# Products and transposes of a fused attention and gated convolution in 32-column strips or whole, after what stands before them, in a new TensorE order

## The chip, the cores and the metric

The kernel runs on one core of a Trainium2 chip. The metric is the device time of one execution in microseconds. Three runs of the kernel before gave 411.37, 413.17 and 414.0 us, so the median is 413.17.

## The reference

Four batches of 12800 rows of 128 channels go through agent attention with 49 agents, and its result through a gated convolution. All arrays are float32.

```python
def sm(a, b):
    s = scale * (a @ b.transpose(0, 2, 1))
    s = s - s.max(-1, keepdims=True)
    e = np.exp(s)
    return e / (e.sum(-1, keepdims=True) + 1e-09)
agent_v = sm(agents, k) @ v              # 49 x 128 per batch
x = sm(q, agents) @ agent_v              # 12800 x 128 per batch
...
for k in range(K):                       # 5 taps, causal
    gate_pre += conv_w[k][None, None, :] * xp[:, k:k + S, :]
gate = 1.0 / (1.0 + np.exp(-gate_pre))
out = gate * (x @ w_val) @ w_out
```

## The kernel before, in words

**Units and chunks.** The keys, values and queries of a batch are cut into 10 units of 1280 rows; the output into 25 chunks of 512 rows per batch, numbered 0 to 100 over the four batches (the last one is split in two). Nothing of `x` is ever written: the agents' values are folded into the weights of the convolution. `x` is a weighted sum over agents, so the gate is a product of the query weights with a folded table (five taps and rests), and so is the value.

**The kinds of work on TensorE**, with the letters of the order table:

- `k` and `q` (`key_scores`, `queries`, through `score_matmuls`, L411): scores of a unit of keys or queries against the agents. They are float32, in column strips: four matmuls of 32 columns (`tile_position=(0, g * BLK)`) take a quarter of the unit each, for two halves of the agents. A float32 matmul stands as two in the trace, so a unit is 16. They write one of two PSUM banks `sc` in turn.
- `v` (`agent_values`, L552): exponentials of the keys' scores times the values, summed in the bank `av`. For batches 1 to 3 they are strips of 32 columns as well, for batch 0 they are 64 columns wide. A unit is 40 matmuls in the trace (20 in batch 0).
- `f` (`fold_weights`, five steps a batch: L606 and L610, L655, L741, L771, L797): normalises the agents' values, multiplies them with `w_val`, splits the results into 16-bit high and low parts in `wst` and `wsp`, and turns them with 16-bit transposes; `wo` is turned as float32 (L771).
- `m`, `n`, `j` (`key_max`, L469 and L484; `regroup`, L521): the maximum over the keys of a batch, turned with two small float32 transposes.
- `t` (`transposes`): turns the query weights `pt` of a unit into `x`. The first four units go through TensorE (L929), the others by a DMA that transposes, issued on SyncE's queue (L915).
- `g` (`gates`, L1008 and L1012): six 16-bit matmuls of 128 columns by 512 rows for a chunk's gate; `a` (`values`, L1035 and L1039): two for its value; `o` (`project`, L1080 to L1082): three for its output.

**Around them.** ScalarE copies key scores out of `sc`, takes exponentials, the tanh `th` of a gate, the 16-bit copy `hh` of `h` and the copy of an output into `ob`. VectorE takes maxima, transposes blocks and makes `h = (th + 1) * val`. GpSimd makes the rest `hl = h - hh` and weighs queries. An out product needs `hh` and `hl` of its chunk.

**What sets the order.** TensorE's order is a table of numbers written out by hand (`order`, L1185 to L1208). The other engines' orders come from `Plan.order`, a list scheduler that runs once over all steps with estimated costs and adds 0.12 us to TensorE's clock wherever the key of a step differs from that of the step before (L153 to L157). Loads go through SyncE's queue into a ring of eleven buffers `ld`, in the order in which the table's `k`, `q` and `v` need them; transposing DMAs, shifted copies (L968) and outputs (L1116) share that queue.

Of the kernel before, what the change touches and what calls it, by code (L numbers as in the profile page):

```python
# [17 lines left out]
P = 128  # L18
G = 4
# [50 lines left out]
class Plan:  # L70
# [25 lines left out]
    def order(self, held=None):  # L96
# [32 lines left out]
        while done < n:  # L129
# [23 lines left out]
            if e == "pe":  # L153
                here += 1
                if key != kind:
                    when += 0.12
                kind = key  # L157
            else:
                queues[e].remove(i)
# [31 lines left out]
def tile_agent_attention_gated_conv(  # L191
# [37 lines left out]
    mrep = const.tile([2, G, BLK], F32, name="mrep")  # L229
# [28 lines left out]
    def small(b):  # L258


        if b:
            return av, "av"
        turn[1] += 1
        return ((outp, "out"), (val, "val"), (gate, "gate"))[turn[1] % 3]

# [35 lines left out]
    nc.vector.memset(fac, 0.0)  # L301
    for t in wst_sb:
        nc.gpsimd.memset(t[:, TAPS + 1 :, :], 0.0)
# [104 lines left out]
    def score_matmuls(b, src, out):  # L408
        for j in range(2):
            for g in range(G):  # L410
                nc.tensor.matmul(  # L411
                    out=out[g * BLK : (g + 1) * BLK, j, 0:GT],
                    lhsT=ag_sb[:, b, j * BLK : (j + 1) * BLK],
                    rhs=src[:, g * GT : (g + 1) * GT],
                    start=True,
                    stop=True,
                    tile_position=(0, g * BLK),
                )
# [35 lines left out]
    def key_max(b, units=range(NU), bias=None):  # L454
# [14 lines left out]
            lambda: nc.tensor.transpose(out=p1[0:2, 0:P], in_=m2, identity=ident),  # L469
# [3 lines left out]
        def spread():  # L473
            rows = p1[0:2, 0:P].rearrange("j (g a) -> j a g", g=G)
            nc.vector.tensor_reduce(
                out=mrep, in_=rows.unsqueeze(1).to_broadcast([2, G, BLK, G]),
                axis=AX.X, op=ALU.max,
            )
# [5 lines left out]
            lambda: nc.tensor.transpose(  # L484
                out=p2[:, 0:2], in_=mrep.rearrange("j g a -> j (g a)"),
                identity=ident[0:2, 0:2],
            ),
# [11 lines left out]
    def regroup(b):  # L499


        p3, at3 = small(b)

        def differ():
            for j in range(2):
                r = slice(j * BLK, (j + 1) * BLK)
                nc.vector.tensor_tensor(
                    out=fac[r], in0=kbias[0][r, j : j + 1], in1=kbias1[r, j : j + 1],
                    op=ALU.subtract,
                )  # L510

        add("dve", 0.25, differ, [("kbias", 0), "kbias1"], ["fac"])
        add(
            "act", 0.2,
            lambda: nc.scalar.activation(out=fac[0:AP_], in_=fac[0:AP_], func=AF.Exp),
            ["fac"], ["fac"],
        )
        yield
        add(
            "pe", 0.2,  # L520
            lambda: nc.tensor.matmul(  # L521
                out=p3[:, 0:1], lhsT=twice,
                rhs=fac, start=True, stop=True,
            ),
            ["fac"], [at3], key="m",
        )
        add("dve", 0.12, lambda: nc.vector.tensor_copy(out=fac2, in_=p3[:, 0:1]), [at3], ["fac2"])

    def agent_values(b, u):
# [5 lines left out]
        cols, key = (BLK, "sc") if b else (AP_, "av")  # L535
# [11 lines left out]

        def matmuls(blocks):
            for n in blocks:
# [37 lines left out]
    def fold_weights(b):  # L587
# [17 lines left out]
        def normals():  # L605
            nc.tensor.matmul(  # L606
                out=pt[:, 0:AP_], lhsT=av2[:, C : C + 1].to_broadcast([P, P]), rhs=fold,
                start=True, stop=True,
            )
            nc.tensor.matmul(  # L610
                out=pt[:, AP_ : 2 * AP_], lhsT=av2[:, 0:C], rhs=fold,
                start=True, stop=True,
            )
# [25 lines left out]
        def gate_scale():  # L639
# [15 lines left out]
            lambda: nc.tensor.matmul(  # L655
                out=pv[:, 0:A], lhsT=wval_sb, rhs=avT, start=True, stop=True
            ),
# [81 lines left out]
        def transposes():  # L739
            for i in range(TAPS + 3):  # L740
                nc.tensor.transpose(  # L741
                    out=pw[:, i * P : (i + 1) * P], in_=wst[:, i, :], identity=ident16
                )
# [27 lines left out]
            lambda: nc.tensor.transpose(out=po[:, 0:P], in_=wo, identity=ident),  # L771
# [23 lines left out]
        def transposes2():  # L795
            for i in range(2):
                nc.tensor.transpose(  # L797
                    out=pq[:, i * P : (i + 1) * P], in_=wsp[:, i, :], identity=ident16
                )
# [107 lines left out]
    def transposes(b, u):  # L907
# [19 lines left out]
        def matmuls():  # L927
            for n in range(NBLK):
                nc.tensor.transpose(  # L929
                    out=ps[:, n // HB, n % HB * P : (n % HB + 1) * P], in_=pt[:, n, :],  # L930
                    identity=ident16,
                )
# [51 lines left out]
    def gates(t):  # L984
# [20 lines left out]
        def matmuls():  # L1005
            for k in range(TAPS):
                c = PAD - HALO + o2 + k
                nc.tensor.matmul(  # L1008
                    out=pg, lhsT=stat[:, k, :], rhs=x1[:, c : c + w],
                    start=(k == 0), stop=False,  # L1010
                )
            nc.tensor.matmul(  # L1012
                out=pg, lhsT=stat[0 : X2K, TAPS + 1, :],
                rhs=x2[0 : X2K, o2 : o2 + w], start=False, stop=True,
# [3 lines left out]
        add("pe", 1.3 * scale, matmuls, xs + x2k + st, [at_g], key="c")  # L1018
# [9 lines left out]
    def values(t):  # L1028
# [5 lines left out]
        def matmuls():  # L1034
            nc.tensor.matmul(  # L1035
                out=pv, lhsT=stat[:, TAPS, :], rhs=x1s[(b * NCH + n0 // CH) // 5 % NX][:, PAD + o2 : PAD + o2 + w],
                start=True, stop=False,
            )
            nc.tensor.matmul(  # L1039
                out=pv, lhsT=stat[0 : X2K, TAPS + 2, :],  # L1040
                rhs=x2[0 : X2K, o2 : o2 + w], start=False, stop=True,
# [25 lines left out]
    def project(t):  # L1067
# [11 lines left out]
        def matmuls():  # L1079
            nc.tensor.matmul(out=po, lhsT=wo16[:, 0, :], rhs=hh, start=True, stop=False)  # L1080
            nc.tensor.matmul(out=po, lhsT=wo16[:, 1, :], rhs=hh, start=False, stop=False)  # L1081
            nc.tensor.matmul(out=po, lhsT=wo16[:, 0, :], rhs=hl, start=False, stop=True)  # L1082

        if w < CH:
            add(
                "pe", 0.1 + 0.86 * scale,
                lambda: nc.tensor.matmul(out=po, lhsT=wo, rhs=h, start=True, stop=True),
# [86 lines left out]
    for t in range(len(chunks) + 2):  # L1174
# [108 lines left out]
```

## Time and profile before

| what | value |
|---|---|
| median of three runs | 413.17 us (411.37 to 414.0) |
| the profiled execution, its own time | 413.01 us |
| its span, first to last instruction | 411.3 us |
| mean granted TensorE clock | 0.994 |
| TensorE matmuls and weight loads in the trace | 3909 each |
| moved by DMA | 126.11 MB, mean 307 GB/s |
| last load used by TensorE | query unit 3.9, at 359.8 us |

A row of the profile names the line of the kernel, the engine (PE is TensorE, PEld its weight loads, DVE VectorE, ACT ScalarE, POOL GpSimd, SPq the queue of SyncE), the operation, what it writes and reads, the shape, a count, and times. `128*32 128x320 f32` is a matmul of 128 rows and 32 columns of the array, which streams 320 float32 columns. A matmul's end is modelled and its start is not, so starts are compared. In a timeline, rows that follow each other and are alike are merged under their first start; in the chain of waits, a piece lasts from its start to the start of the next one on the chain.

### The profile page before, as it was taken

The numbers are of one execution on the slowest core, as the hardware profiler recorded it, in microseconds if no ns is written. First come the engines' busy times: TensorE is split into PE (matmuls) and PEld (weight loads), VectorE is DVE, ScalarE is ACT, GpSimd is POOL, SyncE is SP. The second block draws the span as 40 slices with busy tenths as digits, with TensorE's granted clock in tenths as the row PEclk, the third lists the DMA queues.
The fourth block names the chain that finished last, engine by engine and source line by source line (L and its number), as shares of the span: only waits on it lengthen the run. The fifth ranks groups of instructions, "written<-read, shape, count | busy, mean of one in ns | idle before, by whom it ended". The sixth has DMA issues, their size and how long they took to land.

```text
span 411.3 us, 10037 instructions
## 1 busy us (share of the span) xinstructions
PE 396.3 (96%) x3909; PEld 196.1 (48%) x3909; DVE 259.8 (63%) x488; ACT 296.6 (72%) x523; POOL 286.5 (70%) x368
## 2 busy tenths in 40 slices
PE   4889999999999999999999999999999999999996
PEld 1339534445556444446555544445545544444442
DVE  7878787865777656367672668566756576553222
ACT  1476357778857877869887685798867678788875
POOL 6341558783799987752859594985788899999443
PEclk9989999999999999999999999999999999999999
DMA  8999999899999999999899999999999999996634
GB/s 315 421 416 409 358 380 368 251 288 297 412 335 294 380 300 328 310 362 376 304 272 365 314 390 249 316 223 382 247 382 262 295 251 327 247 228 135 193 124 158
DMA packets 74735, 126.11 MB, mean 307 GB/s; under 512 B 50400, under 2 KB 50784, under 8 KB 74688
## 3 DMA queue, kind: packets, MB, share of 16 engines
q1 hardware_dynamic: 74544, 125.34, 98.6%
q8 instruction: 31, 0.51, 0.5%
q10 hardware_dynamic: 144, 0.13, 0.2%
q14 instruction: 16, 0.13, 0.1%
HBM read 79.25 MB, written 26.21 MB: 256 GB/s over the span
## 4 chain that ended last, share of the span: by engine, by line
PE 88%; DVE 5%; DMA 3%; issue 1%; POOL 1%; ACT 1%; SPq 0%; DVEq 0%; POOLq 0%; ACTq 0%
PE gate L1008 26%; PE sc L411 19%; PE av L552 9%; PE out L1080 6%; PE val L1035 5%; PE val L1039 5%; PE gate L1012 5%; PE out L1081 5%; PE out L1082 5%; DMA ld<-kT 2%; DMA ld<-vP 1%; DVE kmx L446 1%; DVE ob L331 1%; DVE x L306 1%; DVE sT L421 0%
## 5 line engine op out<-in xcount | busy, mean ns | idle before, releaser
L1061 POOL TENSOR_TENSOR hl<-h,hh 128x512 f16<-128x512 f32 x99 | 114.8, 1162 | 61.2 <-ACT hh L1056 60.7
L1008 PE MATMUL gate<-x,stat 128*128 128x512 f16 (+1 forms) x500 | 124.3, 378 | 0.0
L1048 DVE SCALAR_TENSOR_TENSOR h<-th,val 128x512 f32<-128x512 f32 x100 | 68.3, 683 | 70.9 <-PE val L1039 41.4
L411 PE MATMUL sc<-ld,ag_sb 128*32 128x320 f32 x1280 | 99.4, 449 | 8.0 <-DMA ld<-kT 6.0
L1021 ACT ACTIVATE th<-gate,unscale 128x512 f32<-128x512 f32 x100 | 68.5, 685 | 28.0 <-PE gate L1012 22.6
L1101 ACT ACTIVATE ob<-out,oscale 128x512 f32<-128x512 f32 x98 | 67.3, 687 | 22.8 <-PE out L1082 20.2
L1008 PEld LDWEIGHTS <-stat 128*128 128x128 f16 x505 | 47.7, 98 | 61.0 <-issue 6.5
L1056 ACT CAST hh<-h 128x512 f16<-128x512 f32 x99 | 60.6, 613 | 16.1 <-DVE h L1048 15.6
L411 PEld LDWEIGHTS sc<-ld,ag_sb 128*32 128x32 f32 x1280 | 38.5, 112 | 56.1 <-issue 17.8
L829 POOL TENSOR_TENSOR qw<-sT,qmx 128x490 f32<-128x490 f32 x40 | 40.5, 1019 | 33.1 <-DVE qmx L824 32.9
L552 PE MATMUL av<-ld,eT 128*32 128x129 f32 (+1 forms) x1400 | 50.0, 274 | 0.8 <-DMA ld<-vP 0.8
L552 PEld LDWEIGHTS av<-ld,eT 128*32 128x32 f32 (+1 forms) x1400 | 43.7, 113 | 10.2 <-issue 4.7
L421 DVE STREAM_TRANSPOSE sT<-sc 128x640 f32<-128x640 f32 x40 | 33.8, 845 | 21.4 <-PE sc L411 16.6
L437 ACT COPY ks<-sc 128x640 f32<-128x640 f32 x40 | 27.6, 691 | 22.6 <-PE sc L411 14.6
L421 DVE STREAM_TRANSPOSE eT<-e 128x640 f32<-128x640 f32 x40 | 33.3, 839 | 15.9 <-ACT e L543 9.1
L874 POOL TENSOR_TENSOR pt<-qw,pt 128x480 f16<-128x480 f32 x40 | 42.6, 1072 | 0.5 <-ACT pt L860 0.4
L543 ACT ACTIVATE e<-ks,kbias 128x320 f32<-128x320 f32 x80 | 39.6, 552 | 4.0 <-DVE eT L421 3.6
L850 POOL TENSOR_TENSOR qw<-qw,qr 128x480 f32<-128x480 f32 x40 | 39.8, 996 | 3.3
L446 DVE TENSOR_REDUCE kmx<-ks 128x2 f32<-128x640 f32 x38 | 30.3, 805 | 14.8 <-ACT ks L437 14.5
L1035 PE MATMUL val<-x,stat 128*128 128x512 f16 x100 | 37.9, 379 | 0.2 <-DVE h L1048 0.2
L1012 PE MATMUL gate<-x,stat 106*128 106x512 f16 x100 | 38.0, 380 | 0.0
L1039 PE MATMUL val<-x,stat 106*128 106x512 f16 x100 | 37.9, 379 | 0.0
(155 smaller groups left out, 418.0 us busy)
## 6 DMA issues: line engine op xcount, KB each, us to landing
ld<-kT SPq DMA_DIRECT2D x40, 640.0 KB, 9.0
ld<-qT SPq DMA_DIRECT2D x40, 640.0 KB, 9.9
ld<-vP SPq DMA_DIRECT2D x39, 645.0 KB, 11.7
outT<-ob SPq DMA_DIRECT2D x48, 512.0 KB, 6.4
x<-x SPq DMA_DIRECT2D x18, 400.0 KB, 6.6
x<-x SPq DMA_DIRECT2D x4, 200.0 KB, 8.6
outT<-ob SPq DMA_DIRECT2D x3, 256.0 KB, 6.0
ld<-vP SPq DMA_DIRECT2D x2, 322.5 KB, 12.1
```

The source lines that it names most:

```text
L411: nc.tensor.matmul(out=out[g * BLK : (g + 1) * BLK, j, 0:GT], lhsT=ag_sb[:, b, j * BLK : (j + 1) * BLK], rhs=src[:, g * GT : (g + 1) * GT] ...
L421: nc.vector.transpose(out=out.rearrange("p n (j i) -> p j n i", j=2), in_=in_.rearrange("p j (n i) -> p j n i", i=BLK),)
L552: nc.tensor.matmul(out=av[o + j : o + j + cols, 0 : C + 1], lhsT=et[:, n, j : j + cols], rhs=vt[:, n, :], start=(opens and n < 2), stop=(c ...
L1008: nc.tensor.matmul(out=pg, lhsT=stat[:, k, :], rhs=x1[:, c : c + w], start=(k == 0), stop=False,)
L1012: nc.tensor.matmul(out=pg, lhsT=stat[0 : X2K, TAPS + 1, :], rhs=x2[0 : X2K, o2 : o2 + w], start=False, stop=True,)
L1021: lambda: nc.scalar.activation(out=th, in_=pg, func=AF.Tanh, scale=unscale[:, 0:1]),
L1035: nc.tensor.matmul(out=pv, lhsT=stat[:, TAPS, :], rhs=x1s[(b * NCH + n0 // CH) // 5 % NX][:, PAD + o2 : PAD + o2 + w], start=True, stop=False,
L1039: nc.tensor.matmul(out=pv, lhsT=stat[0 : X2K, TAPS + 2, :], rhs=x2[0 : X2K, o2 : o2 + w], start=False, stop=True,)
L1048: lambda: nc.vector.scalar_tensor_tensor(out=h, in0=th, scalar=1.0, in1=pv, op0=ALU.add, op1=ALU.mult),
L1056: "act", 0.18 + 0.43 * scale, lambda: nc.scalar.copy(out=hh, in_=h),
L1061: lambda: nc.gpsimd.tensor_tensor(out=hl, in0=h, in1=hh, op=ALU.subtract),
L1101: lambda: nc.scalar.activation(out=ob[:, o : o + w], in_=po, func=AF.Copy, scale=oscale if w == CH else 1.0),
```

## The change

Three things are changed.

1. A flag `full` says in which form the array was last used: score matmuls and the values of batches 1 to 3 set it to strips, gates and the values of batch 0 to whole. Two helpers, `product` and `turned`, issue a matmul or a transpose whole (128 columns) or as four strips of 32 columns, as the flag stands. Value and out products, folds and the 16-bit transposes go through them; gates do too, but always whole.
2. The float32 transposes of the key maximum and of `wo` become matmuls against the identity; `mrep` is 128 rows high, with zeros below row 2, for that purpose. The first one of the key maximum is a single matmul of 2 columns at tile position (0, 0).
3. In the planner the 0.12 us now falls due only between the keys `sc`, `av` and `g`; the gate's key is `g`. The table that orders TensorE is replaced.

```diff
-                if key != kind:
-                    when += 0.12
-                kind = key
+                if key in ("sc", "av", "g"):
+                    if kind is not None and key != kind:
+                        when += 0.12
+                    kind = key
...
+    full = [False]
+
+    def strips(fn):
+        step = P if full[0] else BLK
+        for j in range(0, P, step):
+            fn(slice(j, j + step), (0, j))
+
+    def product(out, lhsT, rhs, start=True, stop=True):
+        def one(at, place):
+            nc.tensor.matmul(
+                out=out[at], lhsT=lhsT[:, at], rhs=rhs, start=start, stop=stop,
+                tile_position=place,
+            )
+        strips(one)
+
+    def turned(out, in_, identity):
+        def one(at, place):
+            nc.tensor.transpose(
+                out=out[at], in_=in_[:, at], identity=identity, tile_position=place
+            )
+        strips(one)
...
     def score_matmuls(b, src, out):
+        full[0] = False
...
-            lambda: nc.tensor.transpose(out=p1[0:2, 0:P], in_=m2, identity=ident),
+            lambda: nc.tensor.matmul(
+                out=p1[0:2, 0:P], lhsT=m2, rhs=ident, start=True, stop=True,
+                tile_position=(0, 0),
+            ),
...
+            lambda: product(p2[:, 0:2], mrep.rearrange("j g a -> j (g a)"), ident[:, 0:2]),
...
         def matmuls(blocks):
+            full[0] = cols != BLK
...
-            lambda: nc.tensor.transpose(out=po[:, 0:P], in_=wo, identity=ident),
+            lambda: product(po[:, 0:P], wo, ident),
...
         def matmuls():
+            full[0] = True
             for k in range(TAPS):
                 c = PAD - HALO + o2 + k
-                nc.tensor.matmul(
-                    out=pg, lhsT=stat[:, k, :], rhs=x1[:, c : c + w],
-                    start=(k == 0), stop=False,
-                )
+                product(pg, stat[:, k, :], x1[:, c : c + w], start=(k == 0), stop=False)
...
-            nc.tensor.matmul(out=po, lhsT=wo16[:, 0, :], rhs=hh, start=True, stop=False)
-            nc.tensor.matmul(out=po, lhsT=wo16[:, 1, :], rhs=hh, start=False, stop=False)
-            nc.tensor.matmul(out=po, lhsT=wo16[:, 0, :], rhs=hl, start=False, stop=True)
+            product(po, wo16[:, 0, :], hh, stop=False)
+            product(po, wo16[:, 1, :], hh, start=False, stop=False)
+            product(po, wo16[:, 0, :], hl, start=False)
...
-        "f0 g0 k1.1 a0 g1 f0 k1.9 g2 a1 q0.3 q0.5 g3 a2 k1.0 k1.6 q0.6 o0 g4 o1 a3 g5 t0.3 o2 t0.4 "
+        "g0 a0 f0 q0.6 g1 f0 q0.4 g2 o0 a1 g3 q0.5 k1.4 a2 t0.4 q0.8 k1.6 g4 t0.3 t0.8 a3 o2 g6 o1 "
```

**Where the change moves work.** On TensorE in batch 2, around the value product of chunk 49 (`val` reads `x1` and `x2`, `sc` are score units; a row with x8 is one unit, and lines of "..." leave out rows that only repeat). Before, four score units stand together and the value products are whole, on both sides of them:

```order
L1035 MATMUL val_140<-x1_1_105,stat1_130 128x512
L1039 LDWEIGHTS stat1_130
L1039 MATMUL val_140<-x20_108,stat1_130 128x512
L771 MATMUL av_142<-ident_145,wo_184 128x128
L411 MATMUL sc0_137<-ld1_62,ag_sb_148 32x320 x8
L411 MATMUL sc1_138<-ld2_63,ag_sb_148 32x320 x8
L411 MATMUL sc0_137<-ld3_64,ag_sb_148 32x320 x8
L411 MATMUL sc1_138<-ld4_65,ag_sb_148 32x320 x8
L1035 LDWEIGHTS stat0_129
L1035 MATMUL val_140<-x1_2_106,stat0_129 128x512
```

Now the value product of that chunk stands between score units, as two sets of four strips:

```order
L278 MATMUL out_141<-hl1_121,wo161_132 128x512
L440 MATMUL sc1_138<-ld9_70,ag_sb_148 32x320 x8
L278 LDWEIGHTS stat1_130
L278 MATMUL val_140<-x1_1_105,stat1_130 32x512
...
L278 MATMUL val_140<-x20_108,stat1_130 32x512
...
L440 MATMUL sc0_137<-ld10_71,ag_sb_148 32x320 x8
L440 MATMUL sc1_138<-ld0_61,ag_sb_148 32x320 x8
L278 LDWEIGHTS stat0_129
L278 MATMUL gate_139<-x1_2_106,stat0_129 128x512
```

Each of the two strip rows stands four times, with its weight load; the form changes once before and once behind this group, where it changed around every group of score units before.

On TensorE at the key maximum of batch 2 (`m2` is its input), before:

```order
L1012 MATMUL gate_139<-x20_108,stat1_130 128x512
L469 MATMUL av_142<-ident_145,m2_81 2x128
L1035 LDWEIGHTS stat1_130
L1035 MATMUL val_140<-x1_2_106,stat1_130 128x512
...
L484 MATMUL av_142<-ident_145,mrep_82 128x2
```

and now:

```order
L278 MATMUL gate_139<-x21_109,stat1_130 128x512
L498 MATMUL av_142<-ident_145,m2_81 2x128
L278 LDWEIGHTS wo161_132
L278 MATMUL out_141<-hh1_118,wo161_132 128x512
...
L278 MATMUL av_142<-ident_145,mrep_82 128x2
```

It stands between whole products in both; the transposes have become matmuls.

On SyncE's queue late in batch 2 (`x1` from `pt` is a transposing DMA, `vP`, `qT` are loads), before:

```order
L404 DMA ld0_61<-vP 128x1290
L404 DMA ld1_62<-qT 128x1280
L915 DMA_TRANSPOSE x1_2_106<-pt0_100 128x10x128
L915 DMA_TRANSPOSE x1_2_106<-pt1_101 128x10x128
L404 DMA ld2_63<-vP 128x1290
L1116 DMA outT<-ob2_125 128x1024
L404 DMA ld3_64<-vP 128x1290
```

and now:

```order
L931 DMA_TRANSPOSE x1_2_106<-pt0_100 128x10x128
L432 DMA ld9_70<-vP 128x1290
L432 DMA ld10_71<-vP 128x1290
L432 DMA ld0_61<-vP 128x1290
L931 DMA_TRANSPOSE x1_2_106<-pt1_101 128x10x128
L432 DMA ld1_62<-qT 128x1280
L432 DMA ld2_63<-vP 128x1290
L432 DMA ld3_64<-vP 128x1290
```

One query load and two value loads now stand behind the second transpose, where two value loads and an output stood.

More of the change, by code (lines that the diff above doesn't have):

```diff
@@ L228, in tile_agent_attention_gated_conv @@
     m2 = const.tile([P, 2], F32, name="m2")
-    mrep = const.tile([2, G, BLK], F32, name="mrep")
+    mrep = const.tile([P, G, BLK], F32, name="mrep")
     es = ring(2, [P, 2, GT], F32, "e")
@@ L301, in tile_agent_attention_gated_conv @@
     nc.vector.memset(fac, 0.0)
+    nc.vector.memset(mrep, 0.0)
     for t in wst_sb:
@@ L475, in spread @@
             nc.vector.tensor_reduce(
-                out=mrep, in_=rows.unsqueeze(1).to_broadcast([2, G, BLK, G]),
+                out=mrep[0:2], in_=rows.unsqueeze(1).to_broadcast([2, G, BLK, G]),
                 axis=AX.X, op=ALU.max,
@@ L483, in key_max @@
             "pe", 0.2,
[L484 to L487, printed above, removed]
+            lambda: product(p2[:, 0:2], mrep.rearrange("j g a -> j (g a)"), ident[:, 0:2]),
             ["mrep"], [at2], key="m",
@@ L520, in regroup @@
             "pe", 0.2,
[L521 to L524, printed above, removed]
+            lambda: product(p3[:, 0:1], twice, fac),
             ["fac"], [at3], key="m",
@@ L532, in agent_values @@
         vt = ld[i].rearrange("p (n c) -> p n c", c=C + 1)
-        cols, key = (BLK, "sc") if b else (AP_, "av")
         early = b == 0 and u < GROUP1
@@ L546, in exps @@
                 )
+        cols, key = (BLK, "sc") if b else (AP_, "av")
         def matmuls(blocks):
+            full[0] = cols != BLK
             for n in blocks:
@@ L605, in normals @@
         def normals():
-            nc.tensor.matmul(
-                out=pt[:, 0:AP_], lhsT=av2[:, C : C + 1].to_broadcast([P, P]), rhs=fold,
-                start=True, stop=True,
-            )
[L610 to L613, printed above, removed]
+            product(pt[:, 0:AP_], av2[:, C : C + 1].to_broadcast([P, P]), fold)
+            product(pt[:, AP_ : 2 * AP_], av2[:, 0:C], fold)
         add("pe", 0.45, normals, ["av2"], [at_t], key="m")
@@ L654, in fold_weights @@
             "pe", 0.3,
-            lambda: nc.tensor.matmul(
-                out=pv[:, 0:A], lhsT=wval_sb, rhs=avT, start=True, stop=True
-            ),
+            lambda: product(pv[:, 0:A], wval_sb, avT),
             ["avT", "moe"], [at_v], key="m",
@@ L740, in transposes @@
             for i in range(TAPS + 3):
-                nc.tensor.transpose(
-                    out=pw[:, i * P : (i + 1) * P], in_=wst[:, i, :], identity=ident16
-                )
+                turned(pw[:, i * P : (i + 1) * P], wst[:, i, :], ident16)
         add(
@@ L796, in transposes2 @@
             for i in range(2):
-                nc.tensor.transpose(
-                    out=pq[:, i * P : (i + 1) * P], in_=wsp[:, i, :], identity=ident16
-                )
+                turned(pq[:, i * P : (i + 1) * P], wsp[:, i, :], ident16)
         add("pe", 0.25, transposes2, ["wsp"], [at_q], key="m")
@@ L928, in matmuls @@
             for n in range(NBLK):
[L929 to L932, printed above, removed]
+                turned(ps[:, n // HB, n % HB * P : (n % HB + 1) * P], pt[:, n, :], ident16)
         add("pe", 0.65, matmuls, [("pt", g % NPT, n) for n in range(3)], [at], key="t")
@@ L1005, in matmuls @@
         def matmuls():
+            full[0] = True
             for k in range(TAPS):
                 c = PAD - HALO + o2 + k
-                nc.tensor.matmul(
-                    out=pg, lhsT=stat[:, k, :], rhs=x1[:, c : c + w],
-                    start=(k == 0), stop=False,
[L1011 to L1014, printed above, removed]
+                product(pg, stat[:, k, :], x1[:, c : c + w], start=(k == 0), stop=False)
+            product(
+                pg, stat[0:X2K, TAPS + 1, :], x2[0:X2K, o2 : o2 + w], start=False,
             )
         th = ths[t % NT_][:, 0:w]
-        add("pe", 1.3 * scale, matmuls, xs + x2k + st, [at_g], key="c")
+        add("pe", 1.3 * scale, matmuls, xs + x2k + st, [at_g], key="g")
         add(
@@ L1034, in matmuls @@
         def matmuls():
-            nc.tensor.matmul(
-                out=pv, lhsT=stat[:, TAPS, :], rhs=x1s[(b * NCH + n0 // CH) // 5 % NX][:, PAD + o2 : PAD + o2 + w],
-                start=True, stop=False,
-            )
-            nc.tensor.matmul(
-                out=pv, lhsT=stat[0 : X2K, TAPS + 2, :],
-                rhs=x2[0 : X2K, o2 : o2 + w], start=False, stop=True,
+            product(
+                pv, stat[:, TAPS, :],
+                x1s[(b * NCH + n0 // CH) // 5 % NX][:, PAD + o2 : PAD + o2 + w], stop=False,
+            )
+            product(
+                pv, stat[0:X2K, TAPS + 2, :], x2[0:X2K, o2 : o2 + w], start=False,
             )
@@ L1086, in project @@
                 "pe", 0.1 + 0.86 * scale,
-                lambda: nc.tensor.matmul(out=po, lhsT=wo, rhs=h, start=True, stop=True),
+                lambda: product(po, wo, h),
                 [("h", t % NH), "wo"], [at_p], key="c",
```

46 rows, old and new, of the table order are left out of this document.

## The prediction

> **What bounds the kernel now.** I read the sections of the page first, then TensorE's waits, then the chain of waits stretch by stretch. TensorE is the candidate:
>
> ```profile
> PE 396.3 (96%) x3909; PEld 196.1 (48%) x3909; DVE 259.8 (63%) x488; ACT 296.6 (72%) x523; POOL 286.5 (70%) x368
> PE 88%; DVE 5%; DMA 3%; issue 1%; POOL 1%; ACT 1%; SPq 0%; DVEq 0%; POOLq 0%; ACTq 0%
> ```
>
> A busy share says little, since ends of matmuls are modelled. The waits say more (engine, line, what ended the wait, us in total, times, longest):
>
> ```profile
> PE sc L411 <- DMA ld<-kT: 6.0, 1, 6.0
> PE sc L411 <- DVE cmax L376: 1.1, 1, 1.1
> PE gate L484 <- DVE mrep L475: 1.0, 1, 1.0
> PE val L469 <- DVE m L462: 0.8, 1, 0.8
> PE av L552 <- DMA ld<-vP: 0.8, 1, 0.8
> PE sc L411 <- ACT ks L437: 0.7, 2, 0.5
> PE sc L1087 <- DVE h L1048: 0.6, 1, 0.6
> PE out L606 <- DVE av L598: 0.4, 1, 0.4
> PE val L1035 <- DVE h L1048: 0.2, 1, 0.2
> ```
>
> They come to 11.6 us, most of it before the first gate. When that gate starts, and what paces TensorE until then, stands here (start, us, engine, line; first TensorE, then SyncE's queue):
>
> ```profile
> 50.84 1.24 PE L1008 MATMUL gate<-x,stat 128*128 128x512 f16 x5
> 13.83 17.11 SPq L404 DMA_DIRECT2D ld<-vP  x11
> ```
>
> The eleven issues of batch 0's values take 17.11 us, some 1.56 each: the queue lets one go as one lands. The fold needs the last of those values, so up to 50.84 us the loads set the pace, not TensorE's order. Both orders put the same 10 key, 3 query and 10 value units ahead of that fold. From 50.84 to the end TensorE waits about 1.6 us in 360 (vP 0.8, the two for h 0.8). There every nanosecond of its own sequence counts.
>
> What that sequence loses is seen in the chain (start, us, what), where a piece lasts until the next one starts:
>
> ```profile
> 286.56 1.08 PE gate L1008 x5
> 288.29 0.22 PE out L1082
> 291.23 1.10 PE av L552 x40
> 292.33 1.19 PE gate L1008 x5
> 294.39 1.21 PE sc L411 x16
> 296.70 0.32 PE val L1035
> ```
>
> ```profile
> 192.88 1.08 PE sc L411 x16
> ```
>
> Scores and values (L411, L552) are strips: four matmuls of 32 columns side by side. Gates, value and out products are whole, 128 columns. Five gate matmuls take 1.08 us behind whole work and 1.19 behind strips; the first matmul of a value product 0.32, where a whole one in its stream takes 0.22. A score unit takes 1.08 behind strips (192.88) and 1.21 behind whole work. So strips to whole costs 0.10 to 0.11 us, whole to strips 0.13, and the pair **0.24**.
>
> **The change part by part.** *Changes of shape.* I counted them in the order of TensorE's instructions, from the first gate on, as changes of tile width between neighbours: 38 pairs before, 25 after (leaving out the key maximum). 13 pairs by 0.24 is **-3.1 us**. Before the first gate there are fewer changes too; I give them nothing, since the loads pace that part. If that cover were gone, they would be worth a further 0.24 a pair.
>
> *Strips of value and out products.* 17 value products (two matmuls each) and 15 out products (three) become strips: 79 sets of four, each in place of one matmul of 0.22. The trace has no 16-bit strip. Nearest is the score unit: 16 matmuls, four sets of 320 float32 columns, 1.08 us, so 0.27 a set. A whole 16-bit matmul takes 0.216 for 512 columns (1.08 for five), which is the same number of bytes in a partition per us (1280 in 0.27, 1024 in 0.216): four strips side by side stream at full rate. For issue, the nearest is L552: 40 strip matmuls with their weight loads in 1.10 us, 0.11 for a set of four, half of what a set of 512 columns lasts. Bounds per set: no change, or four in a row, 4 x 0.216. The score's row is nearest in kind, so I take 2 ns a set: **+0.2 us**. A gain is excluded, as no strip streams faster than the whole.
>
> [...]
>
> The next two parts rest on these rows (start, us, engine, line, shapes):
>
> ```profile
> 334.88 0.61 PE L741 MATMUL av<-ident,wst 128*128 128x128 f16 x8
> 335.33 0.38 PE L1080 MATMUL out<-hh,wo 128*128 128x512 f16 x1
> 336.41 0.27 PE L771 MATMUL av<-ident,wo 128*128 128x128 f32 x1
> 336.52 1.24 PE L1008 MATMUL gate<-x,stat 128*128 128x512 f16 x5
> ```
>
> *Turned strips.* 20 of the 16-bit transposes (10 blocks of t0.2, 8 of fold 0, 2 of a later fold) become sets of four strips of 128 columns. Whole, eight of them take 0.45 us (334.88 to 335.33), 56 ns each. As strips they are bounded by that from below and by the 0.11 of an L552 set from above: at most 1.1 us in all, of which 18 sets lie before the first gate beside the wait for loads. I count nothing on the path; but fold 0's eight could push the first gate by up to 0.4 if its last load were early.
>
> [...]
>
> *Key maximum and the turning of wo.* These float32 transposes become matmuls against the identity, which run as two passes. L771 now takes 0.11 (336.41 to 336.52); two passes make 0.22: three times after the first gate, **+0.3 us**. The key maximum, three times after the first gate, stands amid whole work in both orders:
>
> ```profile
> 270.59 0.38 PE L1012 MATMUL gate<-x,stat 106*128 106x512 f16 x1
> 270.81 0.27 PE L469 MATMUL av<-ident,m 128*2 128x128 f32 x1
> 270.92 0.38 PE L1080 MATMUL out<-hh,wo 128*128 128x512 f16 x1
> 273.73 0.38 PE L1082 MATMUL out<-hl,wo 128*128 128x512 f16 x1
> 274.04 0.22 PE L484 MATMUL av<-ident,mrep 2*128 2x2 f32 x1
> 274.19 0.39 PE L1035 MATMUL val<-x,stat 128*128 128x512 f16 x1
> ```
>
> L469 starts 0.22 after L1012 and hands on after 0.11: no change of shape is paid. L484, with 2 rows, starts 0.31 after L1082 (0.09 over 0.22) and hands on after 0.15: 0.24 for it, 0.35 for both. After: the first product has one strip and two passes, 2 x 0.11 plus a pair of changes, 0.21 to 0.24; the second is whole, two passes, up to 0.22. Together 0.65, so 0.3 more each, **+0.9 us**; if the lone strip paid no change, +0.2.
>
> ```profile
> L1061 POOL TENSOR_TENSOR hl<-h,hh 128x512 f16<-128x512 f32 x99 | 114.8, 1162 | 61.2 <-ACT hh L1056 60.7
> L1048 DVE SCALAR_TENSOR_TENSOR h<-th,val 128x512 f32<-128x512 f32 x100 | 68.3, 683 | 70.9 <-PE val L1039 41.4
> L1056 ACT CAST hh<-h 128x512 f16<-128x512 f32 x99 | 60.6, 613 | 16.1 <-DVE h L1048 15.6
> ```
>
> *What the new order moves.* Value and out products now stand between score units, and units come in longer runs. Distances that protect TensorE I compared by adding up pieces like those above: a value product to its out product is at least 3.0 us apart in both (last chunk aside), so h, hh and hl (683, 613 and 1162 ns, the groups' means) still fit. SyncE's queue is the tightest: a load stands behind a transpose that waits for GpSimd.
>
> ```profile
> 299.00 11.98 SPq L915 DMA_TRANSPOSE x<-pt  x2
> 311.07 0.54 SPq L404 DMA_DIRECT2D ld<-vP  x1
> 316.46 1.31 PE L552 MATMUL av<-ld,eT 128*32 128x129 f32 x40 [0.75 <-DMA ld<-vP]
> ```
>
> Two transposes hold the queue 12 us, the load goes at 311.07, lands 5.3 later, and TensorE waits 0.75 us. In the new order a query load and two value loads stand behind that second transpose, not two value loads; against this, the query that the transpose belongs to comes some 2 us earlier relative to them. I leave this wait as it is: **0**, bounds -0.8 and +1.6 (one load more, at 1.56).
>
> Sum: -3.1 + 0.2 + 0.3 + 0.9 = **-1.7 us**. The profiled execution took 413.01 us (its span is 411.3, the rest lies outside it); that makes 411.3. The median of the runs shown, 413.17, lies 0.16 above: **411.5 us**. A measurement of this kernel can tell about 1% from no change, that is 4.1 us (below 409.0 or above 417.3).
>
> **The rivals.** *Faster than the sum.* The key maximum pays nothing new, the wait for vP goes, and the first keys' maximum, whose keys are now among the first seven units instead of nine, gives up to 1 us: 413.2 - 3.1 + 0.5 (strips and wo) + 0.2 - 0.8 - 1.0 = **409.0**; any change saved before the first gate takes it under that. Against it: the last values' landing paces that part.
>
> *Loads late.* Ten value, query and key units now follow each other almost unbroken in batch 2, fifteen in batch 1. If at three such runs one transfer more (1.56) is waited for: 411.5 + 4.7 = **416.2**. For it, the 0.75 above; against it, queries and keys are loaded up to eleven units ahead, and gaps without units have become longer too.
>
> *Strips share one stream.* This is the rival on the slow side. The four strips of a value or out product read the same x, hh or hl. If two passes over it were needed, a set would take 0.43: 79 x 0.216 = 17 us, **428.5**. It decides slower from 0.07 us a set on. Against it, L552's strips also share their right side in pairs at full rate.
>
> *It is not the shape.* All strips here are float32 and most whole work is 16-bit, so the 0.24 could belong to the type. Then the 47 changes of type inside the new strip runs would cost, and 50 + 47 stand against 76: 21 x 0.12 = 2.5 more than before, plus 1.4: **417.1**. Against it: L771 is float32 amid 16-bit work and is reached in 0.22; and here a change of shape within float32 costs:
>
> ```profile
> 46.03 0.37 PE L655 MATMUL val<-avT,moe_sb 128*128 128x49 f32 x2
> 46.34 2.54 PE L411 MATMUL sc<-ld,ag_sb 128*32 128x320 f32 x32
> ```
>
> Two passes of L655 take 0.31, where two like L771's one of 0.11, which is wider, would take 0.22.
>
> [...]
>
> **How the numbers follow.** Forecast 0.58, faster than the sum 0.18, loads late 0.16, strips that share one stream 0.05, not the shape 0.03. Faster by over 1%: the half of the second that lies under 409.0 and some of the forecast's lower tail, 0.14. Slower: the shared stream, half of the last, and late loads at more than three places, 0.11. Within 1%: 0.75. The forecast's own range is 410.0 to 413.5 (loads -0.8 to +1.6, key maximum -0.7). Reaching from 1.2 under the faster rival, a few saved changes before the first gate, to the late loads, the range is 407.8 to 416.5.
>
> **What would show it.** Right: units behind value or out strips at 1.08, no 0.32 inside runs of strips, sets of strips 0.22 apart, the first gate within 0.5 us of 50.84, TensorE's waits after it near 1.6 us. Wrong: strip sets of 0.25 or more; waits for ld of over 2 us after the first gate; an extra 0.1 between float32 and 16-bit strips; or a first gate that moves by over 1 us either way, for then the start was not set by the loads.

## The result, and the profile after

The changed kernel takes 418.45 us (median; 417.74 to 418.51), the kernel before beside it 412.88 us (411.37 to 414.0): a ratio of 1.0133, 95% interval 1.0098 to 1.0168. It is slower by 1.3%, outside the predicted range of 407.8 to 416.5. A ratio is worked out from undisturbed runs alone, so it need not be the quotient of two medians. The profiled execution took 417.74 us (span 416.0), against 413.01 (411.3) before: 4.7 us to be found.

The busy time of the engines and the chain of the profile after look much like those of before; TensorE's waits (engine, line, what ended the wait, us in total, times, longest) do not:

```profile
PE 396.2 (95%) x4232; PEld 203.0 (49%) x4232; DVE 259.3 (62%) x489; ACT 296.9 (71%) x523; POOL 286.5 (69%) x368
PE 89%; DMA 5%; DVE 2%; issue 2%; ACT 2%; SPq 0%; DVEq 0%; ACTq 0%
```

```profile
PE sc L440 <- DMA ld<-kT: 6.4, 4, 5.7
PE av L580 <- issue: 3.7, 3, 2.6
PE sc L440 <- DVE kmx L475: 1.7, 1, 1.7
PE av L580 <- DVE m L491: 1.5, 1, 1.5
PE sc L278 <- DVE h L1057: 0.6, 1, 0.6
PE sc L440 <- DMA ld<-qT: 0.6, 2, 0.3
PE gate L278 <- issue: 0.5, 1, 0.5
```

Before, no wait of TensorE was put down to "issue". Here four are, 4.2 us together: TensorE stood still, and nothing that the profile shows held it. All waits for loads (kT, qT) lie ahead of the first gate, none behind it, so "loads late" did not happen. The largest stall, in the order of time (start, us, what; in brackets the idle time ahead and its end):

```profile
116.41 1.26 PE L440 MATMUL sc<-ld,ag_sb 128*32 128x320 f32 x16
117.48 0.62 PE L278 MATMUL val<-x,stat 128*32 128x512 f16 x8
117.92 0.40 PE L580 MATMUL av<-ld,eT 128*32 128x129 f32 x7
120.92 1.32 PE L580 MATMUL av<-ld,eT 128*32 128x129 f32 x33 [2.60 <-issue]
122.17 2.74 PE L278 MATMUL gate<-x,stat 128*128 128x512 f16 x6
124.71 0.84 PE L278 MATMUL out<-hh,wo 128*128 128x512 f16 x2
```

It stands in the middle of a value unit (v1.9): 7 of its 40 matmuls run, and the other 33, on the same tiles, start 2.9 us later. Behind it six gate matmuls last 2.74 us, where six took some 1.46 elsewhere. The windows show why: from 1.00 the granted clock (the column ahead of the last two) falls to 0.60. TensorE's clock record has half speed for 3.41 us there, and 400 to 430 ns for each whole matmul: 1.5 us more.

```profile
117.00:121.00 4.00, 1.40 (x31) 0.67 (x27) 1.05 (x2) 1.13 (x2) 3.58 (x5) 1.00 0.89 225
121.00:125.00 4.00, 4.00 (x40) 1.83 (x40) 2.34 (x5) 0.05 (x1) 1.52 (x3) 0.60 1.51 281
```

In the 3.41 us ahead of the fall (118.36 to 121.77) TensorE stood still for 2.56.

The other three stalls, and the first gate:

```profile
51.20 1.47 PE L278 MATMUL gate<-x,stat 128*128 128x512 f16 x6
...
205.08 0.49 PE L580 MATMUL av<-ld,eT 128*32 128x129 f32 x9 [0.30 <-issue]
210.84 1.02 PE L278 MATMUL gate<-x,stat 128*128 128x512 f16 x4 [0.48 <-issue]
323.51 0.71 PE L580 MATMUL av<-ld,eT 128*32 128x129 f32 x17 [0.85 <-issue]
```

The gate at 51.20 is 0.36 later than before. From start to start the four gaps are 2.87, 0.57, 0.87 and 1.12 us, some 4.9 over what the matmuls there take (0.11 for a set of value strips, 0.22 for a gate matmul).

### The profile page after: what moved, and what is told of

The parts are those of the page before. It is cut to its first block, busy times and chain, and to the rows that moved or that the text cites. A ratio compares the mean times of both kernels' runs of the same rounds, so it can differ in the third digit from the quotient of the medians.

```text
span 416.0 us, 10707 instructions
## 1 busy us (share of the span) xinstructions
PE 396.2 (95%) x4232; PEld 203.0 (49%) x4232; DVE 259.3 (62%) x489; ACT 296.9 (71%) x523; POOL 286.5 (69%) x368
## 4 chain that ended last, share of the span: by engine, by line
PE 89%; DMA 5%; DVE 2%; issue 2%; ACT 2%; SPq 0%; DVEq 0%; ACTq 0%
PE gate L278 32%; PE sc L440 19%; PE out L278 15%; PE val L278 11%; PE av L580 9%; DMA ld<-qT 3%; DMA ld<-kT 2%; DVE eT L450 1%; ACT e L568 1%; PE av L278 1%; PE sc L278 1%; PE av L287 0%; ACT ks L466 0%; DVE h L1057 0%; PE av L498 0%
## 5 line engine op out<-in xcount | busy, mean ns | idle before, releaser
L278 PE MATMUL gate<-x,stat 128*128 128x512 f16 x600 | 147.6, 381 | 0.5 <-issue 0.5
L278 PEld LDWEIGHTS <-stat 128*128 128x128 f16 (+3 forms) x910 | 77.2, 98 | 100.5 <-issue 15.9
L440 PEld LDWEIGHTS sc<-ld,ag_sb 128*32 128x32 f32 x1280 | 40.2, 112 | 54.4 <-issue 19.5
L278 PE MATMUL val<-x,stat 128*128 128x512 f16 (+4 forms) x302 | 60.2, 380 | 0.2 <-DVE h L1057 0.2
L278 PE MATMUL out<-hh,wo 128*128 128x512 f16 (+1 forms) x286 | 59.2, 380 | 0.0
L580 PEld LDWEIGHTS av<-ld,eT 128*32 128x32 f32 (+1 forms) x1400 | 45.0, 113 | 13.1 <-issue 5.6
L278 PEld LDWEIGHTS <-wo 128*128 128x128 f16 (+1 forms) x432 | 30.1, 98 | 32.3 <-issue 2.4
L278 PE MATMUL out<-hl,wo 128*128 128x512 f16 (+1 forms) x143 | 37.6, 378 | 0.0
```

The lines of the kernel that those rows point to most:

```text
L278: nc.tensor.matmul(out=out[at], lhsT=lhsT[:, at], rhs=rhs, start=start, stop=stop, tile_position=place,)
L440: nc.tensor.matmul(out=out[g * BLK : (g + 1) * BLK, j, 0:GT], lhsT=ag_sb[:, b, j * BLK : (j + 1) * BLK], rhs=src[:, g * GT : (g + 1) * GT] ...
L580: nc.tensor.matmul(out=av[o + j : o + j + cols, 0 : C + 1], lhsT=et[:, n, j : j + cols], rhs=vt[:, n, :], start=(opens and n < 2), stop=(c ...
```

## The experiments

**Theory A** came from the DMA part of the profile's page. Queue q8, of kind instruction, moves packets of 16384 bytes (queue, packets, MB); the other one of that kind, q14, moves 16 packets in before and in after. Of the kernel before, of after, and of e6, which has nearly twice the instructions on TensorE:

```profile
q8 instruction: 31, 0.51, 0.5%
```

```profile
q8 instruction: 33, 0.54, 0.5%
```

```profile
q8 instruction: 59, 0.97, 0.9%
```

TensorE issued 7,892, 8,544 and 15,314 instructions (matmuls, weight loads and a few of its sequencer): 28 packets more for 7,422 more, 265 each. From that I estimate a packet at 256 instructions; the stalls below, all 33 at one place of a period of 256, bear that out. In after the packets come one by one from 18.6 to 395.4 us, during the execution, and the page counts their time, like that of the data, as a share of the 16 DMA engines (0.5%). A value unit is 80 instructions in 1.10 us, a score unit 32 in 1.08, a strip product of three 24 in 0.65; a whole gate is 12 in 1.30. The new order has runs of over 500 instructions with no gate. The theory: TensorE runs out of instructions there. **B**: something of the 16-bit strips stops it. **C**: data of the new order are late.

**e1: the new order, all products whole**

```diff
-        step = P if full[0] else BLK
+        step = P
```

> The changed order with value and out products, folds and transposes always whole (no strips but scores and values). Changes of shape after the first gate: 94 instead of 56 (counted as single changes, a pair is two). Theory A (TensorE runs out of instructions inside long runs of units, because its instructions come over the DMA engines in pieces of 256 and a value unit uses 80 of them in 1.1 us): the long runs of units are still there, v1.2 to v1.9 with some 514 instructions instead of 568, so a stall in the middle of a unit with no semaphore behind it remains near 118 us and the time is the changed kernel's 418.4 plus 38 changes of 0.12, 4.6 us, minus at most 2 us of milder stalls: 421 to 423. Rival B (the stall belongs to the 16-bit strips): no stall in the middle of a unit, 418.4 + 4.6 - 6.8 = 416 to 417. Rival C (data that the new order has late): stalls stay and stand at waits for semaphores, 421 to 423 as well, told from A by the waits.

418.9 us, ratio 1.017 (1.0136 to 1.0204). There is no strip left but scores and values, and the stalls are still there, in v1.5 and in v3.1 (1.7 and 2.4 us from start to start). The first of them:

```profile
101.74 1.94 PE L580 MATMUL av<-ld,eT 128*32 128x129 f32 x62
105.12 0.63 PE L580 MATMUL av<-ld,eT 128*32 128x129 f32 x10 [1.45 <-issue]
```

B falls. The time came out 2 us under A's: the stalls after the first gate are 1.1 us less, and the first gate starts 0.8 us earlier, which I had not reckoned with. The half clock is not gone in the profiled execution (420.72 us, mean clock 0.996): it stands for 3.41 us behind the second stall. The other three took 417.7 to 418.93 us at a mean clock of 0.999 to 1.0, which leaves no room for it.

**e2: the strips, the old order**

```diff
-        "k0.3 k0.2 k0.7 k0.0 k0.1 k0.4 k0.5 q0.0 n0 k0.6 k0.9 q0.1 k0.8 n0 q0.2 v0.0 m0 v0.1 m0 "
+        "k0.5 k0.0 q0.1 k0.4 k0.3 k0.8 q0.0 k0.1 k0.2 k0.7 n0 n0 k0.6 k0.9 q0.2 v0.0 m0 v0.1 v0.2 "
...
```

> The changed code (strips by what came before, the key maximum and wo as products) with the order of the kernel before. Changes of shape after the first gate 78 instead of 82 before. Theory A: the runs of units are short, as before, so no stall in the middle of a unit over 0.5 us; time = 412.9 - 4 x 0.12 + 0.2 (strips) + 0.3 (wo) + 0.9 (key maximum) = 413.8, between 413 and 414.5. Rival B (the strips bring the stall): stalls appear in this order too, 416 or more. Rival C (data late in the new order): 413.8 as by A.

421.93 us, ratio 1.0241 (1.0213 to 1.0269): 8 us over A's 413.8, and B's stalls are not there either: a single short one (0.87 from start to start) has no semaphore. The time went to a wait that neither kernel has:

```profile
PE gate L278 <- DMA x<-x: 6.3, 3, 3.0
```

The table sets only TensorE's order. SyncE's queue is ordered by the planner, whose rule the change also alters (0.12 us for a change among scores, values and gates alone, and gates with a key of their own). With the old table and the new rule, x comes late three times, and behind the longest of these waits TensorE's clock is at half for 3.41 us. e5 tests that.

**e3: the long runs cut**

```diff
-... g13 o10 a11 g14 o9 v1.2 t0.9 v1.3 q1.2 q1.1 a12 v1.7 o11 a13 v1.8 q1.3 a14 v1.9 g16 o12
+... g13 o10 a11 v1.2 o9 t0.9 v1.3 g14 q1.2 q1.1 a12 v1.7 o11 a13 g16 v1.8 q1.3 a14 v1.9 o12
...
-... v2.2 v2.7 v2.8 o35 a38 q2.1 v2.4 v2.6 t2.0 g39 t1.9
+... v2.2 v2.7 g39 v2.8 o35 a38 q2.1 v2.4 v2.6 t2.0 t1.9
...
-... v3.8 v3.4 v3.3 q3.3 v3.1 o65 v3.9 o66 t3.2 g70 a68
+... v3.8 v3.4 o65 v3.3 g70 q3.3 v3.1 o66 v3.9 t3.2 a68
```

> The changed kernel with seven places of its order altered: the three long runs of units (v1.2 to v1.9, v2.0 to v2.6, v3.8 to v3.9) are cut by gates that stood just after or before them (g14, g16, g39, g70 with o65). Nothing else is moved. Changes of shape 64 instead of 56, which cost 8 x 0.12 = 1.0 us. Theory A: the 2.8 us stall at v1.9, the half clock behind it (1.5 us) and the 0.5 to 1.0 us stalls of the other two runs shrink to under 0.5 each: 418.4 - 6.0 + 1.0 = 413.4, between 412.5 and 415. Rivals B (strips themselves) and C (late data): the same strips and data are needed in almost the same order, 418 to 419.5.

415.8 us, ratio 1.0092 (1.0063 to 1.0121). The stall of 2.9 us is gone, and so are those at 210.84 and 323.51. One of 1.1 us stays in batch 2, one of 1.7 comes up at 291.5 in a run that was not cut, and cutting moved SyncE's queue again: a wait of 2.2 for x ends at 321.0, and 3.41 us at half clock follow it. The direction is A's, the size is half.

**e4: everything as strips, the old order**

```diff
-        step = P if full[0] else BLK
+        step = BLK
```

(and the table of e2)

> The order of the kernel before, with every value and out product, fold and transpose as four strips; gates stay whole? No: gates go through the same product helper and become strips too, so that after the first gate no change of shape is left (0 instead of 82). TensorE has 15244 instructions instead of 7818. If a change of shape costs 0.12 us and strips stream at full rate, as the trace of the changed kernel says: 412.9 - 9.8 + 0.3 + 0.9 + some 0.5 for strips = 404 to 406, if instructions keep up. Theory A adds: a strip product uses 37 instructions a us instead of 9, so gates no longer let the supply catch up; stalls without a semaphore of 0.5 to 3 us would stand in runs of value units, and the time would be 406 to 416. If the strips cost of themselves (rival B): 415 or more with strip sets over 0.23 apart or stalls in every run. If changes of shape cost nothing: 413 or more without stalls.

427.65 us, ratio 1.0381 (1.0345 to 1.0417), above A's 406 to 416 (B, which gave 415 or more, is answered by e1 and e5); 10.3 us of it are waits for x, as in e2. Ten stalls of over 0.45 us beyond a matmul's own time have no semaphore, and gates and out products have them now too, not value units alone (waits at "issue": av 3.3 us, sc 1.4, out 1.1, val 0.9, gate 0.3): here dense work stalled in all five kinds.

**e5: as e2, with the old planner's rule**

```diff
-                if key in ("sc", "av", "g"):
-                    if kind is not None and key != kind:
-                        when += 0.12
-                    kind = key
+                if key != kind:
+                    when += 0.12
+                kind = key
...
-        add("pe", 1.3 * scale, matmuls, xs + x2k + st, [at_g], key="g")
+        add("pe", 1.3 * scale, matmuls, xs + x2k + st, [at_g], key="c")
```

> The strips of the change with the order of the kernel before AND its planner's rule (0.12 for every change of key, gates keyed as before), so that SyncE's, GpSimd's, ScalarE's and VectorE's queues are exactly those of the kernel before; e2 had the new rule and with it another order of SyncE's queue, and waited 6.3 us for x. Theory D (e2's loss came from the queues that the rule moved): no wait for x; 412.0 - 0.5 (changes) + 0.2 (strips) + 0.3 (wo) + 0.9 (key maximum) = 412.9, between 412 and 414.5 with at most one stall of under 1 us at a boundary of 256 instructions. If the strips themselves disturb the transfers: 418 or more, again with waits for x.

412.84 us, ratio 1.0006 (0.9976 to 1.0035), as expected but for one wait for x that is left:

```profile
PE gate L277 <- DMA x<-x: 0.9, 1, 0.9
```

TensorE's instructions are those of e2, in the same order. The order of the other queues alone is worth 9 us. No stall at "issue" is left. So the strips, the key maximum as products and wo as a product, taken together and less the few changes of shape that they save, cost nothing that can be measured.

**e6: as e5, with everything as strips** (the edit of e4 on e5)

> As e5, but every product, gates too, as four strips: no change of shape after the first gate, 15244 instructions on TensorE. Theory A (TensorE's instructions arrive in pieces of 256, one piece in 5.3 to 7.8 us where stalls stood so far): some 15 stalls without a semaphore, each at the first instruction of a piece (193 modulo 256 in its stream), 8 to 13 us in all as in e4, against 80 changes of 0.12 saved (-9.6) and +1.4 for the rest: 412 to 417. If changes of shape cost nothing and only stalls count: 421 to 426. If instructions were no limit: 404.

420.73 us, ratio 1.0202 (1.0141 to 1.0263): no change of shape after the first gate, and 8 us slower than e5. Its waits:

```profile
PE av L579 <- issue: 3.2, 3, 1.6
PE gate L277 <- issue: 3.0, 3, 1.5
...
PE sc L439 <- issue: 1.2, 2, 0.9
...
PE av L277 <- issue: 1.0, 1, 1.0
```

After the first gate the gaps at the ends of pieces come to 10.9 us. I had expected 412 to 417; of the miss, the first gate (52.05, 1.8 us later than in e5, with two such stalls ahead of it) explains a part, and some 3 us I have not placed.

**e7: 48 instructions more, far ahead**

```diff
     nc.vector.memset(mrep, 0.0)
+    for _ in range(24):
+        nc.tensor.matmul(
+            out=av[:, 0:1], lhsT=ident16, rhs=ident16[:, 0:1], start=True, stop=True
+        )
```

> The changed kernel with 24 one-column matmuls (48 instructions with their weight loads) ahead of the first key, on a bank that is overwritten; order, data, strips and all other queues as in the changed kernel. Theory A: boundaries of pieces fall 48 instructions earlier in the work. The stalls at 120.92 (in v1.9), 205.1, 210.8 and 323.5 are gone from those instructions and stand 48 instructions ahead of them, again at 193 modulo 256; the short pieces then end near 117, 201, 206, 288, 292 and 318 us (times without stalls), and the one near 292 and 288 may stall as well: 418 to 422. Theory B (something in v1.9 or v2.8 themselves, data or loads): stalls stay at the same matmuls of the same units, 418 to 419.

419.4 us, ratio 1.0172 (1.0111 to 1.0232). Nothing else of the program differs from the changed kernel, and the stalls have moved:

```profile
100.80 2.25 PE L584 MATMUL av<-ld,eT 128*32 128x129 f32 x73
105.33 0.42 PE L584 MATMUL av<-ld,eT 128*32 128x129 f32 x7 [2.28 <-issue]
...
118.22 0.73 PE L444 MATMUL sc<-ld,ag_sb 128*32 128x320 f32 x8
120.37 0.74 PE L444 MATMUL sc<-ld,ag_sb 128*32 128x320 f32 x8 [1.42 <-issue]
120.93 0.62 PE L278 MATMUL val<-x,stat 128*32 128x512 f16 x8
```

The stall of v1.9 stands in the query unit ahead of it: counting back from the 8th matmul of v1.9, 7 of that unit, 8 of the value product and 8 of the query's scores are 23 matmuls with their loads, 46 instructions, the sequencer's own left out. Data that v1.9 waits for cannot do that: C falls for these stalls. In the count of TensorE's instructions the four stalls of after stand at 3009, 4545, 4801 and 7361, and e7 stands still at these four counts again, 48 instructions earlier in the work (at the last one the profile names a semaphore, VectorE's transposed scores). Three more counts stall that did not in after: 2497, which is the stall at 105.33 above, 6593 and 6849. So here a shift of the count alone made other pieces come late.

**e8: fewer instructions in the same units**

```diff
+WIDE = {
+    (1, 2), (1, 3), (1, 7), (1, 8), (1, 9), (2, 0), (2, 2), (2, 7), (2, 8), (2, 4), (2, 6),
+    (3, 8), (3, 4), (3, 3), (3, 1), (3, 9),
+}
...
         cols, key = (BLK, "sc") if b else (AP_, "av")
+        if (b, u) in WIDE:
+            cols = AP_
...
-            full[0] = cols != BLK
+            full[0] = b == 0
```

> The changed kernel with 16 value units of its long runs (v1.2, 1.3, 1.7, 1.8, 1.9, 2.0, 2.2, 2.7, 2.8, 2.4, 2.6, 3.8, 3.4, 3.3, 3.1, 3.9) as strips of 64 columns, as batch 0 has them: the same products in the same time, by 40 instructions instead of 80. All other queues are as in the changed kernel. Changes of shape 72 instead of 56, 16 x 0.12 = 1.9 us. Theory A: pieces of 256 last longer there, the four stalls (4.9 us) and the half clock behind the first (1.5) go or shrink under 0.3 each: 418.4 - 6.4 + 1.9 = 413.9, between 413 and 415.5. Theory B or C (data, loads, strips): stalls stay, 419 to 421.

413.75 us, ratio 1.000 (0.9974 to 1.0026): 4.7 us come back with the same order, the same data and the same queues, by 640 instructions fewer, although 16 changes of shape were added. One stall is left (1.77 us from start to start, near 294 us, in a unit that was not made wide):

```profile
PE av L586 <- issue: 1.5, 1, 1.5
```

**e9: wide units chosen by the trace, and the old key maximum**

```diff
+    (1, 0), (1, 1), (1, 4), (1, 5), (1, 6), (1, 7), (1, 8), (2, 3), (2, 4), (2, 6), (2, 7), (2, 8),
+    (3, 3), (3, 4), (3, 5), (3, 6), (3, 7), (3, 8),
...
-            lambda: nc.tensor.matmul(
-                out=p1[0:2, 0:P], lhsT=m2, rhs=ident, start=True, stop=True,
-                tile_position=(0, 0),
-            ),
+            lambda: nc.tensor.transpose(out=p1[0:2, 0:P], in_=m2, identity=ident),
...
```

> The changed kernel with 18 value units of batches 1 to 3 as strips of 64 columns (chosen so that by the changed kernel's own trace no 256 instructions last less than 6.5 us) and the key maximum as the two transposes that it was before. All other queues as in the changed kernel; changes of shape 71 instead of 56. Theory A: no stall at a boundary of 256 instructions over 0.3 us; 418.4 - 4.9 (stalls) - 1.5 (half clock) + 15 x 0.115 (changes) - 0.9 (key maximum) = 412.8, or, from e8, 413.75 - 1.75 (the one stall left there) - 0.9 = 411.1: 410.5 to 413, so at best some 0.3% under the kernel before (412.2). If what e8 gained came from elsewhere than the pieces: 413.5 or more, with stalls.

411.63 us (410.99 to 412.37), ratio 0.9987 (0.9964 to 1.0009). No wait at "issue" is left:

```profile
PE sc L444 <- DMA ld<-kT: 7.9, 4, 5.8
PE av L586 <- DVE m L495: 1.0, 1, 1.0
PE sc L444 <- DMA ld<-qT: 0.7, 3, 0.3
PE sc L282 <- DVE h L1063: 0.6, 1, 0.6
```

A wide unit is 20 matmuls in the time of 40 (1.26 us to the next here, change of shape included; 1.10 for the 40 at 114.94 in e7):

```profile
112.27 1.32 PE L586 MATMUL av<-ld,eT 128*64 128x129 f32 x20
113.53 0.61 PE L282 MATMUL out<-hh,wo 128*32 128x512 f16 x8
```

It is the fastest with the new order, and cannot be told from the kernel before.

**All stalls together.** Counted in the order of issue, in every one of the eleven profiles, after the first gate:

```
                       gaps over 0.45 us with no semaphore   at 193 modulo 256
before                   0                                     -
after                    4                                     4
e1                       2                                     2
e2                       1                                     1
e3                       2                                     2
e4                      10                                    10
e5                       0                                     -
e6                       7                                     7
e7                       6                                     6
e8                       1                                     1
e9                       0                                     -
```

(A gap is taken beyond what a whole matmul or a set of strips takes there. The first TensorE instruction of the trace is number 0.) All 33 stand at the same place of a period of 256, which I take for the first instruction of a piece. In each, TensorE goes on 1.2 to 1.7 us after the end of one 16 KB packet; the packet takes 0.9 to 2.0 us, and starts 2.4 to 5.4 us after TensorE began with the piece ahead of it. From the start of one piece to that of the next, where the next was late, 5.2 to 7.8 us went by: 33 to 49 instructions a us. Value and score units in turn ask for 112 in 2.18 us, 51 a us.

## Why the prediction was wrong, point by point

**The step that failed** is "What the new order moves". It compared distances between products and asked SyncE's queue for late loads, and closed with "I leave this wait as it is: 0". It saw the longer runs ("ten value, query and key units now follow each other almost unbroken in batch 2, fifteen in batch 1"), and asked of them only whether data come in time. It did not ask whether instructions do, though the page of before shows the queue that brings them. In the profiled execution that is 4.9 us of stalls, shown by e7 (they move with the instruction count), e8 and e9 (they go with fewer instructions) and the table, and 1.5 us of half clock behind the longest of them.

**The terms of the sum.** *Changes of shape*: 13 pairs fewer, as counted. In the trace after, a score unit follows a whole product in 0.310 us and a strip product in 0.196; a whole product follows a score in 0.365, a strip in 0.249: 0.23 a pair, -3.0 us (forecast 0.24, -3.1). *Strips*: sets of four 16-bit strips come 0.216 apart, whole matmuls 0.217: 0.0, forecast +0.2. The four strips of a set start 23 ns apart from first to last (117.484 to 117.507), but the next set starts 0.216 behind it all the same. *Turned strips*: nothing on the path, as forecast; the upper bound of 0.11 a set was not reached, since ten sets take 0.56 us, 0.056 each as when whole (rows below). *wo*: two passes 0.11 apart, +0.3, as forecast. *Key maximum*: the first product costs 0.40 over its neighbours (0.306, 0.109 and 0.204 from start to start, less 0.217), the second 0.14; before, 0.11 and 0.25. So +0.2 each, +0.6 in all, forecast +0.9; the second, now whole, costs less than the transpose of two rows that it replaces. *Queue*: the wait of 0.75 for vP is gone, -0.8, within its bounds. *First gate*: +0.4, forecast 0.

The turned strips in the trace after:

```profile
46.18 0.74 PE L287 MATMUL sc<-ident,pt 128*32 128x128 f16 x40
46.74 0.27 PE L278 MATMUL val<-avT,moe_sb 128*32 128x49 f32 x8
```

**The account**, of the profiled executions: 413.0 + 0.4 (first gate) - 3.0 + 0.3 + 0.6 - 0.8 + 4.9 (stalls) + 1.5 (half clock) + 0.5 (a wait for eT at 203.7 us) = 417.4, measured 417.74; 0.3 us stay open.

**The rivals.** "Loads late" gave 416.2, not far off by luck: no load was late. Strips did not share a stream by halves: a set came 0.216 behind the one ahead of it, not 0.43. "It is not the shape" gave 417.1, the nearest figure, by luck as well: here it was the shape, not the type, as a score starts 0.195 to 0.196 after a 16-bit strip of an out product, and so does the next 16-bit strip (0.196). "Faster than the sum" had two of its three gifts (the key maximum nearly, the vP wait), and lost them to the stalls. The forecast's own four signs of "right" nearly all came true (units behind strips 1.08, sets 0.22 apart, first gate within 0.5), except the one that decided: TensorE's waits after the first gate.

What stays open is why a packet starts as late as 5.4 us after the piece ahead of it was begun, where 2.4 to 3.5 occurs as well. Ahead of the stalls at 120.92 and 205.08, the packets (118.57 and 202.51) started as a transposing transfer of 256-byte packets ended (118.8 and 202.7); by those before 210.84 and 323.51 (208.36, 320.88) none ran. No run took the transfers away.

## What to carry to other kernels

Count instructions as well as matmuls: where a change makes an engine's work denser, or takes the sparse work out of a dense run, hold the shortest time of 256 instructions against the 5.2 to 7.8 us that went by here where a piece was late, and try wider tiles where four strips can be two (e8 gained 4.7 us so). A wait put down to "issue" in the middle of a group on the same tiles (2.60 us in v1.9) was the sign here; its place in the instruction count told it from late data (e7). A planner's rule that orders the other queues has to be tried apart from the table that it was made with.

## What was not expected of the hardware

- A change of tile shape cost 0.114 to 0.116 us in each direction, in after between 32 and 128 columns (0.310 instead of 0.196, 0.365 instead of 0.249), in the runs with wide units also between 32 and 64 (score to value unit 0.363 instead of 0.249, back 0.203 instead of 0.088). That is so whether the type changes (the first two) or not (the last two).
- In after, four strips of 32 columns streamed 512 columns of 16 bits as fast as one matmul of 128 (216 and 217 ns).
- In before and after the granted clock changes only at whole steps of 3.413 us from the start of its record (in after at the 4th, 5th, 33rd, 34th and 119th), and behind the first gate it went with how much of a step TensorE stood still, not with how long the stall was. Five steps with 2.09 us or more of standstill, by the profile's modelled ends (e3 2.09, e1 2.15, e2 2.22, after 2.56, e4 3.41), were each followed by one at half clock. None with 1.85 or less was: in e7 the stall of 2.55 us fell into two steps, with 1.85 in the fuller one, and in e4 a wait of 3.32 us with 1.55 in the fuller one. Ahead of the first gate the edge is less sharp: in before, 1.80 was followed by half clock as well.
- The same instructions on TensorE with another order of the other queues (e2 and e5) differ by 9 us.
